# 32 instead of 24 attention score units formed ahead, in the same twelve steps

## The chip, the core and the metric

The kernel runs on one core of a Trainium2 chip. The metric is the device time of one execution in microseconds (us), as the median of several runs. The engines are TensorE (PE; its weight loads are shown apart as PEld), VectorE (DVE), ScalarE (ACT), GpSimd (POOL) and SyncE (SP, which here issues DMAs).

## What is computed

Three layers in a row, in float32: attention that keeps the 32 largest scores of each row, a mixture of eight experts whose gates are balanced by eight rounds of row and column normalisation, and a feed-forward layer with the Mish function. Cut to what matters here:

```python
# q, k, v: (2 batches, 8 heads, 576 tokens, 64)
scores = scale * np.matmul(q, k.transpose(0, 1, 3, 2))
kth = np.partition(scores, -32, axis=-1)[..., -32:-31]
scores = np.where(scores >= kth, scores, -1e9)
attn = np.exp(scores - np.max(scores, axis=-1, keepdims=True))
attn = attn / (np.sum(attn, axis=-1, keepdims=True) + 1e-09)
x = np.matmul(attn, v)             # then as 1152 tokens x 512
for e in range(8):                 # the experts, P is the balanced gate
    out += P[:, e:e + 1] * (np.maximum(x @ w1[e], 0.0) @ w2[e])
y = mish(out @ w_in) @ w_out
```

## The kernel before

The 1152 tokens are nine tiles of 128. A unit is one tile and one head (t, h), so there are 72 units, numbered 0 to 71 in order of tiles. Tiles 0 to 3 belong to the first batch, 5 to 8 to the second, tile 4 to both. A unit goes through these functions, each some steps later than the one before:

- `scores` multiplies the queries with the keys into PSUM (L227; four matmuls of 288 columns, eight for tile 4) and ScalarE copies the result to SBUF as tile `s` (L236, one copy of 576 columns), which has six buffers.
- `threshold`, two steps on, finds the 32 largest on VectorE with four MAX8 (L255) and three MATCH_REPLACE8 (L262); ScalarE takes the exponential (L273).
- `mask`, three steps on, multiplies by the mask on VectorE (L291). The first 13 units do this otherwise, with a part on GpSimd (L286, L287).
- `norm` divides by the sum: VectorE forms the reciprocal (L300, L301), ScalarE scales (L306).
- `values` turns the result on TensorE (L326, L337), ScalarE copies it (L329, L340), and TensorE multiplies with the values (L349, L356).

`attention` writes all this into a plan, a list of calls for each step; step i begins with the scores of unit i. The 24 units of `EARLY` have their scores formed ahead: all heads of tiles 2 and 3 and heads 0 to 3 of tiles 5 and 6, two in a step from step 5 to step 16, as the last calls of the step. Such a score has two PSUM banks (`mm1`, shared with the experts' first product), one for each half of 288 columns, and ScalarE copies each half (L240). The first ten units are left in SBUF tiles that are not used yet. The rest (`k >= 10`) go through an SBUF tile with two buffers, named `away`, to DRAM (L446), and are read back into an `s` tile when their turn comes (L210). `fetch`, two steps before the first unit of a half tile, loads its keys (`load_k`) and its queries (`load_q`: DMA L182, a copy to float32r on ScalarE L187, the remainder by subtraction on GpSimd L189). The query tiles `q1` and `q2` have three buffers, handed out in the order in which the loads are written.

The stages: tiles 0 and 1 alone go first. Then the experts' work on tiles 0 and 1 (c0 in the names) and tiles 2 and 3 (c1) is woven with attention on tiles 2 to 8: a generator of expert matmul groups runs, and after each group the attention generator is advanced as far as its step allows (a quarter of a step for each group). One turn ends at each `yield`; `scores` gives one where it forms scores, and none where they are there already. Last come the experts on tiles 4 to 8 (c2) and the feed-forward layer (d). An expert's piece is loaded by SP (L518, three buffers), split by ScalarE (L521) and GpSimd (L523), used by the first product (L620) and the second (L597), with hh by ScalarE (L538) and hl by VectorE (L539) between them.

TensorE's order is that of the program. The other engines' orders, SP's queue among them, are fixed when the program is built, by priorities and a planner's times. On the chip each engine works through its list in order.

Of the kernel before, what the change touches and what calls it, by code (L numbers as in the profile page):

```python
# [20 lines left out]
B, H, S, D = 2, 8, 576, 64  # L21
HG = 4
# [22 lines left out]
LAG2 = 2  # L45
AHEAD = 2
POOL_UNITS = 13
EARLY = [(t, h) for t in (2, 3) for h in range(H)] + [(t, h) for t in (5, 6) for h in range(HG)]
EARLY_FROM, EARLY_PER_STEP = 5, 2
HOLD, RATE = 8, 0.25  # L50
FILL_FROM = 11

# [21 lines left out]
def attention_moe_moe2(ctx: ExitStack, tc: tile.TileContext, qT, kT, vm, vt, wg, wst, w64, out):  # L74
# [74 lines left out]
    def load_k(b, h):  # L149


        raw = sp.tile([P, S], F32, tag="kraw", name=f"kraw_{b}_{h}", bufs=2)
        nc.sync.dma_start(raw, kT[b, h])
        k = kp.tile([P, S], F32R, tag="ks", name=f"ks_{b}_{h}")
        step, eng = (HS, nc.vector) if (b, h) == (0, 0) else (S, nc.gpsimd)
        for c in range(0, S, step):
            cols = slice(c, c + step)
            nc.scalar.activation(k[:, cols], raw[:, cols], AF.Copy)
            eng.tensor_sub(k[D:, cols], raw[D:, cols], k[D:, cols])
        ks[b, h] = k  # L160
# [32 lines left out]
    def queries(t, g):  # L193
        if (t, g) not in qset:
            qset[t, g] = load_q(t, g)
        return qset[t, g]

    def scores(t, h, store=None):

        if store is None and h % HG == 2:  # L200
            nt, ng = (t, 1) if h < HG else (t + 1, 0)
            if nt < NT and (nt, HG * ng) not in EARLY:
                with st("attn"):
# [200 lines left out]
    def attention():  # L404
        with st("attn"):
            load_k(0, 0)
            queries(0, 0)
            load_k(0, 1)
            wgraw = const.tile([P, NC, E], F32, name="wgraw")
            nc.sync.dma_start(wgraw, wg)  # L410
            nc.gpsimd.tensor_copy(wgs[:, :, :E], wgraw)
            nc.gpsimd.tensor_sub(wgs[:, :, E : 2 * E], wgraw, wgs[:, :, :E])
        units = [(t, h) for t in range(NT) for h in range(H)]
        plan = {}
        for u, (t, h) in enumerate(units):
            pooled = u < POOL_UNITS
            for order, (stage, delay) in enumerate(
                (
                    (scores, 0),
                    (partial(threshold, on_pool=pooled), AHEAD),  # L420
                    (partial(mask, on_pool=pooled), AHEAD + 1),
                    (partial(norm, on_pool=pooled), AHEAD + (2 if pooled else 1)),
                    (values, AHEAD + (3 if pooled else 2)),
                )
            ):
                plan.setdefault(u + delay, []).append((order, u, partial(stage, t, h)))
        stores = {}

        def early(t, h):

            k = EARLY.index((t, h))
            if k < 2:
                x = xfirst.tile([P, S], F32, tag=("xh1", "xl1")[k], name=f"early{k}")
            elif k < 10:
                name = ("xh2", "xl2")[(k - 2) // 4]
                if (k - 2) % 4 == 0:
                    stores[name] = xlast.tile([P, 4, S], F32, tag=name, name=f"early_{name}")
                x = stores[name][:, (k - 2) % 4, :]
            else:
                with st("attn"):  # L440
                    x = sp.tile([P, S], F32, tag="away", name=f"early{k}", bufs=2)
            yield from scores(t, h, x)
            if k >= 10:
                with st("attn"):
                    away[t, h] = dram.tile([P, S], F32, tag=f"away_{t}_{h}", name=f"away_{t}_{h}")
                    nc.sync.dma_start(away[t, h], live.pop(("s", t, h)))  # L446

        def fetch(t, h):
            with st("attn"):
                for b in range(t * P // S, (t * P + P - 1) // S + 1):  # L450
                    for i in range(h, h + HG):
                        if (b, i) not in ks:
                            load_k(b, i)
                queries(t, h // HG)
            yield from ()

        for k, (t, h) in enumerate(EARLY):
            step = EARLY_FROM + k // EARLY_PER_STEP
            plan[step].append((9, k, partial(early, t, h)))
            if h % HG == 0:  # L460
                plan[step - 2].append((8, k, partial(fetch, t, h)))
        for i in sorted(plan):
            runs = [run for _, _, run in sorted(plan[i], key=lambda x: x[:2])]
            blocks = 2 if i % 2 else 4
            for k, _ in enumerate(chain.from_iterable(run() for run in runs)):
                yield i + min(k + 1, blocks) / blocks
# [198 lines left out]


    at = attention()
    for _ in at:
        if live.get("done") == CHUNKS[0][-1]:
# [191 lines left out]
```

## Time and profile before

| | us |
|---|---|
| median of 3 runs | 1226.93 |
| lowest and highest | 1226.42, 1229.37 |
| the profiled execution | 1226.21 |
| its span, first to last instruction | 1224.4 |
| granted TensorE clock, mean share of full speed | 0.994 |

| engine | busy us | share of the span |
|---|---|---|
| TensorE (matmuls) | 1172.0 | 96% |
| weight loads | 1040.0 | 85% |
| VectorE | 858.1 | 70% |
| ScalarE | 652.7 | 53% |
| GpSimd | 540.1 | 44% |

The shares are means over stages that differ. A busy TensorE is not one at its peak, since matmuls are pipelined and their records overlap. The profile leaves out the numbers of buffers, so units are told apart by counting the instructions of a line in their order.

### The profile page before, as it was taken

What the parts mean: (1) busy time and instruction counts of PE and PEld (TensorE: products, weight loads), DVE (VectorE), ACT (ScalarE), POOL (GpSimd) and SP (SyncE); (2) the same over time, 40 slices, a digit from 0 to 9 for tenths busy, and PEclk for the clock granted to TensorE, in tenths of its full rate; (3) what the DMA queues carried; (4) which work ended last, traced back from release to release, by engine and by line L of the source; (5) the groups of instructions that cost most, each with busy time, mean ns of one, the idle gap of its engine ahead of it and who ended that gap; (6) DMA issues with size and microseconds to landing.
All of it is one profiled execution on the core that took longest, in us unless ns stands there. A gap on an engine that the chain in (4) does not pass through costs nothing.

```text
span 1224.4 us, 20740 instructions
## 1 busy us (share of the span) xinstructions
PE 1172.0 (96%) x7267; PEld 1040.0 (85%) x7267; DVE 858.1 (70%) x1857; ACT 652.7 (53%) x1289; POOL 540.1 (44%) x424
## 2 busy tenths in 40 slices
PE   2777999999999999999999999999999999999998
PEld 1556888988889898889899999999999998889997
DVE  7999999999999999713656867777666632323221
ACT  5786777877777777664223333333333333444432
POOL 7844778877777777773112112121121122221210
PEclk9899999999999999999999999999999999999999
DMA  8444555575655554665225655655444331233201
GB/s 257 125 136 148 177 173 174 171 227 179 212 165 157 163 158 155 198 220 159 69 82 186 197 190 166 213 182 188 138 139 154 118 98 62 94 95 113 77 27 43
DMA packets 105113, 183.18 MB, mean 150 GB/s; under 512 B 14128, under 2 KB 24624, under 8 KB 105008
## 3 DMA queue, kind: packets, MB, share of 16 engines
q1 hardware_dynamic: 103712, 180.68, 47.4%
q8 instruction: 57, 0.93, 0.3%
q10 hardware_dynamic: 1296, 1.18, 0.3%
q14 instruction: 48, 0.39, 0.1%
HBM read 158.55 MB, written 23.27 MB: 148 GB/s over the span
## 4 chain that ended last, share of the span: by engine, by line
PE 80%; DVE 15%; DMA 2%; ACT 1%; POOL 1%; issue 1%; SPq 0%; POOLq 0%; ACTq 0%
PE h_c2e L620 18%; PE y_c2e L597 18%; PE h_d L620 8%; PE y_d L597 8%; PE y_c0e L597 7%; PE h_c0e L620 7%; DVE top L255 6%; DVE w L262 5%; PE h_c1e L620 4%; PE y_c1e L597 4%; DVE em L291 2%; PE pv L349 2%; PE tr L326 1%; DMA kraw<-in_kT_dram 1%; PE sc L227 1%; PE pv L356 1%
## 5 line engine op out<-in xcount | busy, mean ns | idle before, releaser
L523 POOL TENSOR_TENSOR wl_c2e<-wraw_c2e,wh_c2e 128x512 fp32r<-128x512 f32 x64 | 84.0, 1312 | 344.3 <-ACT wh_c2e L521 344.3
L523 POOL TENSOR_TENSOR wl_c0e<-wraw_c0e,wh_c0e 128x512 fp32r<-128x512 f32 x128 | 171.6, 1356 | 53.7 <-ACT wh_c0e L521 50.8
L523 POOL TENSOR_TENSOR wl_c1e<-wraw_c1e,wh_c1e 128x512 fp32r<-128x512 f32 x128 | 172.7, 1373 | 51.2 <-ACT wh_c1e L521 48.2
L521 ACT ACTIVATE wh_c2e<-wraw_c2e 128x512 fp32r<-128x512 f32 x128 | 81.0, 633 | 172.9 <-PE y_c2e L597 100.6
L255 DVE MAX8 top<-w 128x8 f32<-128x576 f32 x216 | 158.2, 750 | 0.8
L620 PE MATMUL h_c2e<-xh,wh_c2e 128*128 128x320 f32 x512 | 158.2, 309 | 0.0
L620 PE MATMUL h_c2e<-xl,wh_c2e 128*128 128x320 f32 x512 | 158.0, 309 | 0.0
L620 PE MATMUL h_c2e<-xh,wl_c2e 128*128 128x320 f32 x512 | 158.0, 309 | 0.0
L539 DVE SCALAR_TENSOR_TENSOR hl_c2e<-h_c2e,hh_c2e 128x320 fp32r<-128x320 f32 x128 | 62.6, 489 | 98.1 <-ACT hh_c2e L538 97.9
L597 PE MATMUL y_c2e<-wh_c2e,hh_c2e 128*128 128x512 f32 x320 | 126.9, 397 | 0.0
L597 PE MATMUL y_c2e<-wh_c2e,hl_c2e 128*128 128x512 f32 x320 | 125.7, 393 | 0.0
L597 PE MATMUL y_c2e<-wl_c2e,hh_c2e 128*128 128x512 f32 x320 | 125.1, 391 | 0.0
L523 POOL TENSOR_TENSOR wl_d<-wraw_d,wh_d 128x512 fp32r<-128x512 f32 x32 | 41.4, 1294 | 161.0 <-ACT wh_d L521 161.0
L521 ACT ACTIVATE wh_c0e<-wraw_c0e 128x512 fp32r<-128x512 f32 x128 | 80.5, 629 | 52.6 <-PE y_c0e L597 21.0
L262 DVE MATCH_REPLACE8 w<-top,w 128x576 f32<-128x576 f32 x144 | 106.7, 743 | 0.0
L558 DVE TENSOR_TENSOR hl_d<-mg_d,hh_d 128x320 fp32r<-128x320 f32 (+1 forms) x48 | 31.6, 658 | 96.0 <-ACT hh_d L557 96.0
L620 PEld LDWEIGHTS h_c2e<-xl,wh_c2e 128*128 128x128 f32 x512 | 96.1, 188 | 2.7
L620 PEld LDWEIGHTS h_c2e<-xh,wh_c2e 128*128 128x128 f32 x512 | 96.0, 188 | 2.3
L620 PEld LDWEIGHTS h_c2e<-xh,wl_c2e 128*128 128x128 f32 x512 | 96.0, 188 | 0.0
L538 ACT ACTIVATE hh_c2e<-h_c2e 128x320 fp32r<-128x320 f32 x128 | 54.9, 429 | 76.5 <-PE h_c2e L620 75.4
L521 ACT ACTIVATE wh_c1e<-wraw_c1e 128x512 fp32r<-128x512 f32 x128 | 80.1, 628 | 28.7 <-PE y_c1e L597 12.3
L521 ACT ACTIVATE wh_d<-wraw_d 128x512 fp32r<-128x512 f32 x64 | 40.4, 632 | 95.8 <-PE y_d L597 40.9
(170 smaller groups left out, 3313.4 us busy)
## 6 DMA issues: line engine op xcount, KB each, us to landing
wraw_c0e<-in_wst_dram SPq DMA_DIRECT2D x128, 256.0 KB, 3.0
wraw_c1e<-in_wst_dram SPq DMA_DIRECT2D x128, 256.0 KB, 3.0
wraw_c2e<-in_wst_dram SPq DMA_DIRECT2D x128, 256.0 KB, 3.0
cx<-in_w_dram SPq DMA_DIRECT2D x32, 512.0 KB, 4.0
wraw_d<-w SPq DMA_DIRECT2D x64, 256.0 KB, 2.6
yd<-ysp SPq DMA_DIRECT2D x32, 256.0 KB, 3.6
yb<-yd SPq DMA_DIRECT2D x32, 256.0 KB, 3.2
w<-cc SPq DMA_DIRECT2D x32, 256.0 KB, 3.4
```

Of the source, the lines that this page charges most:

```text
L227: nc.tensor.matmul(halves[half], q[:, h % HG, :], ks[b, h][:, half * HS : (half + 1) * HS], start=(i == 0), stop=(i == len(terms) - 1),)
L255: top8 = nc.vector.max(g, src)
L262: nc.vector.match_replace(w, g, src, NEG)
L291: nc.vector.scalar_tensor_tensor(em, s, kth, e, op0=ALU.is_ge, op1=ALU.mult, accum_out=sm)
L349: nc.tensor.matmul(pv[i * D : (i + 1) * D, pair, c0:c1], vmain[b, pair][:, i, c, :], live["at", i][:, c, c0:c1], start=(c == 0), stop=False,)
L521: nc.scalar.activation(hi, raw, AF.Copy)
L523: eng.tensor_sub(lo, raw, hi)
L538: nc.scalar.activation(h, ps, AF.Relu)
L539: live["hl"] = nc.vector.scalar_tensor_tensor(l, ps, 0.0, h, op0=ALU.max, op1=ALU.subtract)
L558: nc.vector.tensor_sub(l, g, h)
L597: nc.tensor.matmul(y, h[:, j * P : (j + 1) * P], w, start=(f == 0 and k == 0), stop=(f == nf - 1 and k == 2),)
L620: nc.tensor.matmul(ps, w[:, c * P : (c + 1) * P], x[:, c, c0 : c0 + m], start=(k == 0), stop=(k == 3 * NC - 1),)
```

## The change

Heads 0 to 3 of tiles 7 and 8 join the list, which makes 32 units. They are spread over the same twelve steps, 5 to 16, by 3, 3, 2 in turns instead of two in each. The new ones have `k >= 24`, so they go to DRAM as units 10 to 23 do. The keys that they need are those of tiles 5 and 6; two more query loads come to the first stage, and are no longer made later. The steps of the older units shift: `fetch` for tile 5 is called in step 9 instead of 11, for tile 6 in step 10 instead of 13, and for tiles 7 and 8 in steps 12 and 13.

```diff
-EARLY = [(t, h) for t in (2, 3) for h in range(H)] + [(t, h) for t in (5, 6) for h in range(HG)]
-EARLY_FROM, EARLY_PER_STEP = 5, 2
+EARLY = [(t, h) for t in (2, 3) for h in range(H)] + [(t, h) for t in (5, 6, 7, 8) for h in range(HG)]
+EARLY_FROM, EARLY_STEPS = 5, 12
@@ attention
         for k, (t, h) in enumerate(EARLY):
-            step = EARLY_FROM + k // EARLY_PER_STEP
+            step = EARLY_FROM + k * EARLY_STEPS // len(EARLY)
             plan[step].append((9, k, partial(early, t, h)))
             if h % HG == 0:
                 plan[step - 2].append((8, k, partial(fetch, t, h)))
```

## Rows read from the trace of the kernel before

**Rows 1.** The page: span, then busy tenths in 40 equal slices.

```profile
span 1224.4 us, 20740 instructions
...
PE   2777999999999999999999999999999999999998
...
DVE  7999999999999999713656867777666632323221
```

**Rows 2.** Stretches: us; busy PE, PEld, DVE, ACT, POOL (instructions); clock; DMA.

```profile
33.00:57.00 24.00, 16.82 (x85) 13.46 (x86) 23.77 (x59) 17.86 (x40) 22.51 (x17) 0.80 0.52 150
...
57.00:100.00 43.00, 31.21 (x216) 25.05 (x215) 43.00 (x113) 37.66 (x91) 18.18 (x16) 0.95 0.43 142
...
380.00:500.00 120.00, 119.05 (x863) 106.26 (x862) 119.06 (x282) 89.67 (x178) 90.92 (x67) 1.00 0.53 161
```

**Rows 3.** TensorE's waits, 120 us to the end: total us, times, longest; first and last.

```profile
PE tr L337 <- ACT at L329: 0.8, 1, 0.8
...
PE h_c1e L620 <- DVE hl_c1e L539: 0.2, 1, 0.2
```

**Rows 4.** Lines L306 and L326: duration ns min/median/max, first and last start.

```profile
L306 ACT ACTIVATE em<-em,r x72: 758/768/819, 29.8 to 511.9; 128x576 f32<-128x576 f32 x72
...
L326 PE MATMUL tr<-ident,em x288: 270/272/476, 30.6 to 522.6; 128*128 128x128 f32 x144
```

**Rows 5.** Timeline: start us, us, engine, line, operation; units 39 and 55.

```profile
288.39 0.77 ACT L306 ACTIVATE em<-em,r 128x576 f32<-128x576 f32 x1
...
289.70 0.66 PE L326 MATMUL tr<-ident,em 128*128 128x128 f32 x4 [0.24 <-ACT at L329]
...
394.18 0.76 ACT L306 ACTIVATE em<-em,r 128x576 f32<-128x576 f32 x1
...
410.48 0.60 PE L326 MATMUL tr<-ident,em 128*128 128x128 f32 x4
```

**Rows 6.** The chain that ended last, 490 to 500 us: start us, us, what.

```profile
493.22 0.54 PE sc L227 x4
...
496.97 0.53 PE sc L227 x4
```

**Rows 7.** The page's DMA issues: count, KB each, median us to landing.

```profile
s<-away SPq DMA_DIRECT2D x14, 288.0 KB, 4.1
```

**Rows 8.** ScalarE's groups, 57 to 100 us: count | busy us, mean ns | idle before.

```profile
L240 ACT ACTIVATE early<-sc 128x288 f32<-128x288 f32 x28 | 10.6, 417 | 1.1 <-ACT early L240 0.7 <-PE sc L227 0.3
...
L187 ACT ACTIVATE q<-qraw 128x512 fp32r<-128x512 f32 x7 | 4.4, 625 | 0.0
```

**Rows 9.** TensorE's longest wait, 57 to 100 us: total us, times, longest.

```profile
PE sc L227 <- ACT early L240: 8.7, 9, 2.2
```

**Rows 10.** Timeline: copies of two early units of one step.

```profile
81.05 0.72 ACT L240 ACTIVATE early<-sc 128x288 f32<-128x288 f32 x2
...
83.07 0.69 ACT L240 ACTIVATE early<-sc 128x288 f32<-128x288 f32 x2
```

**Rows 11.** Timeline: a query load's two halves.

```profile
68.96 0.62 ACT L187 ACTIVATE q<-qraw 128x512 fp32r<-128x512 f32 x1
...
69.72 2.74 POOL L189 TENSOR_TENSOR q<-qraw,q 128x512 fp32r<-128x512 f32 x2 [3.57 <-ACT q L187]
```

**Rows 12.** Timeline: the end of the first stage.

```profile
90.59 0.65 ACT L236 ACTIVATE s<-sc 128x576 f32<-128x576 f32 x1
...
91.82 0.75 DVE L255 MAX8 top<-s 128x8 f32<-128x576 f32 x1
...
97.79 0.84 PE L227 MATMUL sc<-ks,q 128*128 128x288 f32 x4 [0.86 <-ACT early L240]
...
100.90 1.58 PE L349 MATMUL pv<-at,vm 128*64 128x128 f32 x16 [0.84 <-ACT at L329]
...
104.74 0.66 PE L326 MATMUL tr<-ident,em 128*128 128x128 f32 x4 [1.41 <-ACT em L306]
...
107.40 0.36 PE L620 MATMUL h_c0e<-xh,wh_c0e 128*128 128x256 f32 x1
```

## The prediction

> **What bounds the kernel now.** I read the page first, then the stretches, then who waited for whom on TensorE, then the chain. The slices [rows 1] show two regimes. Up to slice 4 (about 107 us) VectorE is full and TensorE is not; from then to the end TensorE is full, and VectorE beside it as far as slice 16 (about 500 us). The stretches say it in numbers [rows 2]: from 57 to 100 us VectorE is busy 43.00 of 43, ScalarE 37.66, TensorE 31.21; from 380 to 500 us TensorE has 119.05 of 120 and VectorE 119.06. Two engines at 99% do not tell which sets the pace, so I looked at waits: from 120 us to the end TensorE has five kinds of wait, from 0.8 us down to 0.2, together 2.6 us [rows 3]. It has also a reserve against VectorE. The last of the 72 normalisations (L306) begins at 511.9 and lasts 0.77; the last of the four transposes that need it (L326) starts at 522.6 [rows 4]. VectorE's and ScalarE's result is there some 9.5 us early. For tile 6's last head (unit 55, counted in order) it is 410.48 less 394.94, 15.5 us [rows 5]. So after 107 us TensorE sets the time, with VectorE 10 to 15 us ahead; before it VectorE does, with ScalarE close behind.
>
> **What leaves the long stretch.** The eight units are heads 0 to 3 of tiles 7 and 8. Each is four matmuls of 288 columns. On the chain a unit takes 0.54 and 0.53 us from its first matmul to the next work [rows 6] (their "busy" adds up to more, since pipelined matmuls overlap). 8 x 0.535 = 4.3 us come off TensorE between about 390 and 470 us. Eight copies to SBUF and two query loads leave ScalarE and GpSimd there too, for which TensorE did not wait; I count them at nothing. If VectorE were not ahead, none of the 4.3 would come through: the reserve of 9.5 to 15.5 us is the cover. What is late next is VectorE.
>
> **What comes back there.** Eight reads of 288 KB on SP's queue replace the copies. A read waits for a free one of six `s` buffers, and behind it in SP's queue stand the weight loads. The fourteen such reads of before are of the same kind, land in a median 4.1 us [rows 7], and left no wait on TensorE for weights [rows 3]. Bounds: a gain is excluded, since nothing waited for the copies; a weight load held up by one read is 4 us late at most, with three buffers ahead of it. I take nothing, by the fourteen.
>
> **What the moved scores call forth.** A score that returns at once yields no turn to the weaving of attention into the experts, so the transposes of odd units come earlier by about a step; and four stored units arrive together, so VectorE interleaves more units and the older ones end later. Before shows this at heads 4 to 7 of tile 4, while the four stored units of tile 5 were due: the normalisation of unit 39 begins at 288.39, its transposes at 289.70 [rows 5], a reserve of 0.5 us where unit 55 has 15.5. So such a group takes some 15 us of reserve for a moment, and the units ahead of tiles 7 and 8 have about that. Bounds: 0, to 4.3 us of waits (the whole gain); I take 0.3, since the wait at unit 39 was 0.24 [rows 5], and since a TensorE that arrives later (next part) gives reserve back.
>
> **What enters the first stage.** Steps 5 to 16 take 3, 3, 2 units by turns instead of 2: up to step 8 that is 11 instead of 8, from step 9 on 21 instead of 16. ScalarE pays most: a unit is two copies of 0.417 us, 0.83, and the two query loads (now here) 0.625 each [rows 8]. From 33 to 57 us three units add 2.5 us to 17.86 of 24 [rows 2]: covered. From 57 to 100 us five units and two query copies add 4.15 + 1.25 = 5.4 us to 37.66 of 43: 43.06, no idle time left. GpSimd gets two subtractions of 1.3 us and has room (18.18 of 43). SP gets eight more writes, each of which waits in its queue for two copies.
>
> Does the end of the stage move? TensorE works in order, and its early scores have two PSUM banks for two halves: the second unit of a step waits for the copies of the first. From 57 to 100 us it waited 8.7 us for these copies alone [rows 9], so here it walks at ScalarE's pace. Lower bound: the 5.4 us fill the 5.3 idle us, shift 0. Middle: ScalarE keeps the share it reached, 37.66 / 43 = 0.876, and 5.4 / 0.876 = 6.2 us are added. Upper bound: each of five third units costs TensorE a whole round trip, as from the copies at 81.05 to those at 83.07 [rows 10], 2.0 us, so 10; and a query buffer adds to it. There are three; the loads' order becomes (5,0) before (1,1), so (5,0) gets the buffer that head 3 of tile 1 still reads in step 11, and is itself wanted in step 11. The trace shows what refilling costs: the copy begins at 68.96, GpSimd's part at 69.72 and it is 1.3 us long [rows 11]; some 2 us, with one unit's transposes (0.5) to cover them, so 1.5. Lag at most 11.5.
>
> The tail takes some of it back. Between the last early score (97.79) and the experts' first matmul (107.40) TensorE waits 0.84 + 1.41 = 2.2 us for the last units [rows 12]; a late TensorE finds them done. Shift = 6.2 - 2.2 = 4.0 us; from both sides 0 to 9.3. I take the middle, for the stretch reached no more than 0.876 while TensorE stood waiting for it. VectorE should lose less: it takes a unit 0.6 us after its score is copied (90.59 + 0.65, then 91.82), but that unit is transposed only at 104.74 [rows 12], 13 us later for some 6 us of work (43 us make about 7.5 units), so older work lies beside it.
>
> **The sum.** Profiled execution 1226.21 (span 1224.4 and 1.8 around it): -4.3 + 4.0 + 0.3 = 0.0, so 1226.2. The median of the runs shown is 0.7 above the profiled one: 1226.9, in round numbers 1227.
>
> Here a rule speaks against the change. The Trainium skill (Perfetto Trace Analysis, Identifying the Most-Contended Engine) takes occupancy as a fair measure of how close VectorE is to its limit, and not for TensorE's matmuls. By it VectorE's 119.06 of 120 would make it the engine to relieve from 380 to 500 us, and taking scores off TensorE there would give nothing. The reserve of 9.5 to 15.5 us speaks against it, as far as 4.3 us go.
>
> **The rivals.** *Faster:* the copies fit in ScalarE's idle time and the shift is 0: 1226.9 - 4.3 = 1222.6. For it: 5.3 us idle against 5.4. Against: engines in order that wait for each other seldom fill every gap. 0.18.
>
> *Slower, first stage:* round trips and the query buffer set TensorE's lag, 11.5 us, shift 9.3. It decides once the lag passes the 2.2 us of tail and the 4.3 us of gain, 6.5 us. Time 1226.9 - 4.3 + 9.3 = 1231.9. For it: the waits for copies [rows 9]. Against: ScalarE's backlog shrinks when TensorE is slower. 0.20.
>
> *VectorE is the pace from 380 to 500 us:* waits before the transposes take the 4.3 back, and the first stage's 4.0 stay: 1226.9 + 4.0 = 1230.9. For it: unit 39. Against: no wait over 0.8 us now. 0.09.
>
> That the change does not do what it says: the units can only be moved, but a read that lands late would make VectorE wait where ScalarE's copy came in time; this is inside the third rival's price.
>
> **How the numbers follow.** Forecast 1227 (0.53), faster 0.18, the two slower ones 0.29. The measurement tells about 0.3%, 3.7 us, so "same" is 1223.2 to 1230.6; the faster case lies just below it, the slower ones just above. Range 1222 to 1233, a microsecond beyond the outer cases.
>
> **What would show it.** Right: L236 falls from 48 copies to 40 and L240 rises from 48 to 64; the experts' first matmul starts near 111 us instead of 107.4; ScalarE is above 90% from 57 us to the last early copy; from there to the end TensorE's way is some 4 us shorter, with waits near 3 us. Wrong towards faster: first matmul at 107 to 108. Wrong towards slower: past 114 us, with longer waits for early copies or query loads; or waits of several us before L326 near 400 and 465 us. The forecast fails altogether if the engines' static order, which is planned anew for the whole program, comes out different elsewhere.

## The result and the profile after

The changed kernel takes 1236.28 us (median of 6 runs, 1232.91 to 1237.51); the kernel before, run beside it, 1227.73 (6 runs, 1226.42 to 1229.37). The ratio is 1.0070, 95% interval 1.0057 to 1.0083: slower by 8.6 us. I had forecast 1227 with a range of 1222 to 1233, so the time lies outside it, on the slower side. The profiled execution of the changed kernel is the fastest of its six, 1232.91 (span 1231.1); the trace shows 6.7 us of the 8.6.

The page of the changed kernel, as in [rows 1], with TensorE's granted clock below:

```profile
span 1231.1 us, 20808 instructions
...
PE   3777999999999999999999999999999999999998
...
DVE  7999999899999999823656777777666632323221
PEclk9888999999999999999999999999999999999999
```

The stretches of [rows 2] again: us; busy PE, PEld, DVE, ACT, POOL (instructions); granted clock; DMA share; GB/s.

```profile
33.00:57.00 24.00, 18.50 (x94) 13.98 (x92) 23.58 (x60) 19.65 (x45) 23.22 (x18) 0.86 0.52 146
57.00:100.00 43.00, 30.96 (x175) 24.60 (x174) 40.98 (x99) 34.85 (x82) 16.98 (x14) 0.84 0.40 136
380.00:500.00 120.00, 119.10 (x874) 105.97 (x873) 119.41 (x291) 89.36 (x175) 93.79 (x69) 1.00 0.61 192
```

From 57 to 100 us more work was planned, and less gets done: TensorE runs 175 matmuls where it ran 216, VectorE 99 instructions for 113, ScalarE 82 for 91. ScalarE's busy time falls from 37.66 to 34.85 of 43 us. The stage did not fill up; it became slower.

The end of the first stage on TensorE, against [rows 12] (timeline: start us, us, engine, line, operation, what it waited for):

```profile
104.23 0.53 PE L227 MATMUL sc<-ks,q 128*128 128x288 f32 x2 [2.03 <-ACT early L240]
105.05 2.29 PE L227 MATMUL sc<-ks,q 128*128 128x288 f32 x6 [0.29 <-ACT early L240]
...
112.45 0.83 PE L227 MATMUL sc<-ks,q 128*128 128x288 f32 x4 [0.35 <-ACT early L240]
113.12 1.04 PE L326 MATMUL tr<-ident,em 128*128 128x128 f32 x8
...
115.21 1.58 PE L349 MATMUL pv<-at,vm 128*64 128x128 f32 x16 [0.94 <-ACT at L329]
...
120.14 0.37 PE L620 MATMUL h_c0e<-xh,wh_c0e 128*128 128x256 f32 x1
```

The same stretch on ScalarE: unit 15's score is copied, and later an early copy waits for a store:

```profile
101.82 0.65 ACT L236 ACTIVATE s<-sc 128x576 f32<-128x576 f32 x1
...
110.56 0.71 ACT L240 ACTIVATE early<-sc 128x288 f32<-128x288 f32 x2 [1.56 <-DMA away<-early]
```

And on VectorE, unit 15's first maximum:

```profile
102.51 0.76 DVE L255 MAX8 top<-s 128x8 f32<-128x576 f32 x1
```

The experts' first matmul starts at 120.14 in place of 107.40, 12.7 us late. Unit 15's score is copied at 101.82 in place of 90.59, and VectorE takes it at once. From the experts' first matmul to the end of the span the way is 1231.1 - 120.1 = 1111.0 us; before it was 1224.4 - 107.4 = 1117.0. So the trace reads: +12.7 in the first stage, -6.0 behind it.

Behind it, TensorE's waits from 120 us to the end, as in [rows 3]:

```profile
PE tr L326 <- ACT at L329: 1.6, 4, 0.9
PE h_c0e L620 <- DVE hl_c0e L539: 1.1, 1, 1.1
PE cs L493 <- DVE gate L489: 0.2, 1, 0.2
```

L306 and L326, with the columns of [rows 4]:

```profile
L306 ACT ACTIVATE em<-em,r x72: 756/769/808, 28.2 to 518.1; 128x576 f32<-128x576 f32 x72
...
L326 PE MATMUL tr<-ident,em x288: 270/272/474, 29.0 to 528.8; 128*128 128x128 f32 x144
```

The timeline at unit 55, as in [rows 5]:

```profile
414.12 0.76 ACT L306 ACTIVATE em<-em,r 128x576 f32<-128x576 f32 x1
...
415.43 0.66 PE L326 MATMUL tr<-ident,em 128*128 128x128 f32 x4 [0.90 <-ACT at L329]
```

And the reads among the DMA issues, as in [rows 7]:

```profile
s<-away SPq DMA_DIRECT2D x22, 288.0 KB, 4.1
```

The waits sum to 2.9 us against 2.6. Unit 55, now followed by four stored units, has its reserve cut to 415.43 - 414.88 = 0.55 us, and what TensorE then waits for, 0.90 us, is ScalarE's copy of transposes (L329). The last unit's reserve is as before. The 22 reads land in the same median 4.1 us as the 14 did.

### The profile page after: what moved, and what is told of

It is laid out like the page before. It is cut to its first block, busy times and chain, and to the rows that moved or that the text cites. A ratio compares the mean times of both kernels' runs of the same rounds, so it can differ in the third digit from the quotient of the medians.

```text
span 1231.1 us, 20808 instructions
## 1 busy us (share of the span) xinstructions
PE 1180.0 (96%) x7267; PEld 1045.0 (85%) x7267; DVE 858.9 (70%) x1857; ACT 656.7 (53%) x1298; POOL 545.3 (44%) x425
## 4 chain that ended last, share of the span: by engine, by line
PE 89%; DVE 3%; ACT 3%; DMA 3%; POOL 1%; issue 1%; SPq 0%; ACTq 0%; POOLq 0%
PE h_c2e L620 18%; PE y_c2e L597 18%; PE h_d L620 8%; PE y_d L597 8%; PE h_c0e L620 7%; PE y_c0e L597 7%; PE h_c1e L620 7%; PE y_c1e L597 7%; PE pv L349 3%; PE tr L326 2%; PE sc L227 2%; DMA kraw<-in_kT_dram 1%; DVE top L255 1%; PE pv L356 1%; DVE w L262 1%
## 5 line engine op out<-in xcount | busy, mean ns | idle before, releaser
L523 POOL TENSOR_TENSOR wl_c0e<-wraw_c0e,wh_c0e 128x512 fp32r<-128x512 f32 x128 | 174.3, 1373 | 48.3 <-ACT wh_c0e L521 41.7
L620 PE MATMUL h_c2e<-xh,wh_c2e 128*128 128x320 f32 x512 | 158.3, 309 | 0.0
L620 PE MATMUL h_c2e<-xl,wh_c2e 128*128 128x320 f32 x512 | 157.9, 308 | 0.0
L620 PE MATMUL h_c2e<-xh,wl_c2e 128*128 128x320 f32 x512 | 157.8, 308 | 0.0
L620 PEld LDWEIGHTS h_c2e<-xh,wh_c2e 128*128 128x128 f32 x512 | 96.0, 188 | 2.5
L620 PEld LDWEIGHTS h_c2e<-xl,wh_c2e 128*128 128x128 f32 x512 | 96.0, 188 | 2.3
L227 PE MATMUL sc<-ks,q 128*128 128x288 f32 x320 | 69.3, 350 | 29.6 <-ACT early L240 12.1
L620 PEld LDWEIGHTS h_c2e<-xh,wl_c2e 128*128 128x128 f32 x512 | 96.0, 188 | 0.0
```

The costliest lines, as they stand in the source:

```text
L227: nc.tensor.matmul(halves[half], q[:, h % HG, :], ks[b, h][:, half * HS : (half + 1) * HS], start=(i == 0), stop=(i == len(terms) - 1),)
L523: eng.tensor_sub(lo, raw, hi)
L620: nc.tensor.matmul(ps, w[:, c * P : (c + 1) * P], x[:, c, c0 : c0 + m], start=(k == 0), stop=(k == 3 * NC - 1),)
```

## The experiments

Unless another base is named, an edit is made to the changed kernel. A "third unit" is the third early unit of a step that has three; there are eight. "First matmul" is the experts' first matmul (L620) in the run's profiled execution.

**Gain and price apart.** First the eight units' forming is left out of the kernel before.

```
+SKIPPED = [(t, h) for t in (7, 8) for h in range(HG)]
...
+        at_ = (t - 2, h) if (t, h) in SKIPPED else (t, h)
+        if at_ in away:
...
+                nc.sync.dma_start(s, away[at_])
```

> The kernel before, without forming the scores of heads 0 to 3 of tiles 7 and 8 at all: the stored scores of tiles 5 and 6 are read a second time in their place, so these eight units work on other scores. The first stage is that of before. If TensorE is the pace from 380 to 500 us: 4.3 us under before, 1223.4. If VectorE is: no change, 1227.7. With waits before the transposes near 400 and 465 us: between, 1224 to 1227.

1223.33 us, ratio 0.9972 [0.9961, 0.9983]: -3.4 us. First matmul 108.9, from there to the end 1111.5. The gain is there, though VectorE is as busy as before (119.54 of 120 us from 380 to 500 us). Then the price without the gain:

```
...
-        if (t, h) in away:
+        if (t, h) in away and t < 7:
```

(with the queries of tiles 7 and 8 loaded a second time)

> The changed kernel, but the eight new units, formed ahead and stored, are formed again in their place (with their query loads), and the stored ones are never read. Pays the whole price in the first stage and gains nothing after it: if gain and price simply add, 4.3 us over the changed kernel, 1240.6; the experts' first matmul near 120 us as in the changed kernel. If the late start hides something later, less.

1237.88, ratio 1.0089 [1.0069, 1.0109]: +10.9 us; first matmul 121.4. Gain and price add up to 7.5 of the measured 8.6 us, which the intervals allow.

**Is it the number of units, or their density?** Only 24 units, as before, but in nine steps:

```
+EARLY = [(t, h) for t in (2, 3) for h in range(H)] + [(t, h) for t in (5, 6) for h in range(HG)]
+EARLY_FROM, EARLY_STEPS = 5, 9
```

> The 24 units of before at the density of the changed kernel: 3, 3, 2 in turns over nine steps instead of two in each of twelve. If the number of units in a step is what hurts (round trips through two PSUM banks), TensorE falls behind in these nine steps by some 5 us and has three empty steps to catch up: first expert matmul 108 to 110 us, time 1228 to 1230. If the total amount of work hurts, as before: 1227.7. If a query buffer wanted in the step that frees it hurts, it is here too (tile 5 in step 11): up to 2 us.

1233.87, ratio 1.0058 [1.0039, 1.0077]: +7.1 us with not one matmul or copy more than the kernel before. First matmul 115.9. From 57 to 100 us (columns as above):

```profile
57.00:100.00 43.00, 32.49 (x171) 26.27 (x171) 39.69 (x97) 32.74 (x79) 18.08 (x16) 0.74 0.42 141
```

ScalarE is busy 32.74 of 43 us, and TensorE needs 32.49 us for 171 matmuls where before it needed 31.21 for 216. So more work is not needed for the cost; three to a step suffice, and they cost more than the 1228 to 1230 us that I had named. One thing comes with them in this run as in the change: `fetch` is called for tile 5 in step 9 and for tile 6 in step 10, in place of 11 and 13. No run has three to a step without these sooner loads.

Next all 32, two to a step, over sixteen steps (`EARLY_STEPS` 16):

> The 32 units, but two to a step over sixteen steps, so that no step has a third. Where a step with two early units takes what it took before, the first stage ends its two tiles as before (first matmul of the experts near 107 us in place of 120.1), and the last eight units stand in the steps behind it, beside the experts, where they cost TensorE about what they save later: 1224 to 1229 us. Were the price one of the number of early units, wherever they stand (stores, reads, ScalarE's copies): 1233 us or more. By the theory of the third unit (24 units in 9 steps have 6 thirds and cost 7.1 us, the 8 units with no gain have 8 thirds and cost 10.9 us: 1.2 to 1.4 us for each) the price is zero.

1235.22, ratio 1.0061 [1.0045, 1.0077]. ScalarE's timeline where unit 15's score is copied:

```profile
90.24 0.65 ACT L236 ACTIVATE s<-sc 128x576 f32<-128x576 f32 x1
```

TensorE's timeline at the first matmul:

```profile
112.60 0.37 PE L620 MATMUL h_c0e<-xh,wh_c0e 128*128 128x256 f32 x1
```

And TensorE's wait for early copies from 105 to 180 us (total us, times, longest):

```profile
PE sc L227 <- ACT early L240: 4.8, 4, 2.1
```

With two to a step unit 15 is copied at 90.24 us, as in the kernel before (90.59), and its normalisation is on time as well (103.92 before). The transposes that need it are not (104.74 before):

```profile
103.86 0.78 ACT L306 ACTIVATE em<-em,r 128x576 f32<-128x576 f32 x1
...
108.89 1.05 PE L326 MATMUL tr<-ident,em 128*128 128x128 f32 x4
```

So half of my theory held, up to unit 15's score. Behind it the early units that are left stand ahead of the last transposes in TensorE's order, with 2.1 of the 4.8 us of waits, and the first matmul is 5.2 us late. The last of them stand beside the experts, where I had expected them to cost no more than they save; the way from the first matmul to the end is 1120.4 us, longer than the kernel before's 1117.0. The time is in the range of the rival that I had named, a price of each early unit wherever it stands. Beginning two steps sooner instead (`EARLY_FROM, EARLY_STEPS = 3, 14`):

> The 32 units over fourteen steps, beginning two steps sooner: four steps of a third unit in place of eight. Theory of the third unit: 4 x 1.2 to 1.4 us of price less the gain of 3.4 us: 1228 to 1230 us, with the first matmul of the experts near 112 to 114 us. Rival, that the amount of work in the first stage sets its length: as the change, 1235 to 1238 us. A second rival: the sooner start takes keys and ScalarE from the first units, which at 22 to 37 us wait for their keys, and costs more there: over 1238 us.

1236.28, ratio 1.0068; first matmul 122.2. The time lies in the range of the first rival. The trace shows what the second one named: TensorE's waits from 20 to 60 us are now for keys (1.9 us in the changed kernel). So this run cannot tell what four third units in place of eight are worth.

```profile
PE sc L227 <- POOL ks L159: 16.7, 2, 11.7
```

**One resource at a time.** Each of the next takes away one thing on which TensorE or ScalarE was seen to wait. Four tiles instead of two for the stores:

```
+                    x = sp.tile([P, S], F32, tag="kraw" if k >= 16 and k % 2 else "away", name=f"early{k}", bufs=2)
```

> The changed kernel with four SBUF tiles instead of two for the units on their way to DRAM (from unit 16 of the list on, every second one uses the two tiles through which keys come in). ScalarE's waits for a store to land (2.8 us in the changed kernel) go. If they set the lag: 5 us or more come back, 1231 or less. If not: 1234 to 1237.

1236.19, ratio 1.0069. ScalarE's waits from 33 to 115 us; first the one for stores in the changed kernel:

```profile
ACT early L240 <- DMA away<-early: 2.8, 3, 1.6
```

The same view of this run:

```profile
ACT em L306 <- DVE r L301: 3.8, 3, 1.6
...
ACT early L240 <- DMA away<-early: 0.9, 1, 0.9
```

The wait for stores goes from 2.8 to 0.9 us, a wait for VectorE of 3.8 us that the changed kernel does not have there takes its place, and the first matmul is at 120.1 as before. Query buffers of their own (the queries of tiles 5 and 8 in `yp` tiles):

> The changed kernel, but the queries of tiles 5 and 8 go to two tiles that are free in the first stage, so no query load waits for a buffer that is read in the step that needs it. If the two late query loads (copies at 74.8 and 101.3 us in the changed kernel) set the lag: 3 to 5 us come back, 1231 to 1233. If not: 1235 to 1237.

1237.47, ratio 1.0072; first matmul 120.1. Every other early unit through the PSUM banks `sc` of the ordinary scores, with one copy in place of two:

> The changed kernel, but every second early unit is formed in the two banks of the main scores and leaves PSUM in one copy of 576 columns instead of two of 288. If the round trip through the two banks sets TensorE's lag, most of the 13 us of the first stage go, first expert matmul at 108 to 112 us, time 1224 to 1229. If it is the landing of the stores, the query buffers or the clock, the first matmul stays past 116 us and the time above 1232.

1237.18, ratio 1.0080; first matmul 122.5. The same in the kernel before, as a control:

> The kernel before (24 units, two in each step) with every second early unit in the banks of the main scores and one copy for it. In before VectorE sets the end of the first stage, so faster early scores should bring 0 to 1 us: 1226.7 to 1227.7. If the round trips cost time there too, TensorE's lag of 4 to 7 us in the middle of the stage goes and up to 2 us come back.

1227.88, ratio 1.0001. Every other early unit in the two banks that hold the odd transposes (`tag=("mm1", "mm2")[store_k % 2]`):

> The change, with every other early unit's scores formed in the two PSUM banks that hold the odd transposes, so that TensorE can run two units ahead of ScalarE's copies in place of one. If the two banks are what ties TensorE to the copies: TensorE's waits for early copies between 57 and 115 us (14, 11.2 us) fall to under 4 us and the time to 1226 to 1231 us. If it is ScalarE's order (the copies stand behind exponentials and norms that wait for VectorE), waits move from copies to copies and the time stays at 1235 to 1238 us.

1240.27, ratio 1.0104, worse. The waits of scores for early copies fall from 10.8 us in the changed kernel (13 times in this window; the 11.2 named above belong to a longer one) to 7.2, and the transposes wait for the same copies instead (57 to 115 us):

```profile
PE tr L326 <- ACT early L240: 8.8, 3, 4.5
PE sc L227 <- ACT early L240: 7.2, 10, 1.5
```

The first of the three placed right behind the step's own scores (order 0.5 in place of 9):

> The change, with the first of the three units of a step placed right behind the step's own scores, ahead of its transposes and products, instead of all three last. If the lag comes from three hand-offs of TensorE and ScalarE in a row at the end of a step, it falls: 1227 to 1233 us, the score of unit 15 written before 99 us in place of 102.5. If it is the number of early units in a step, wherever in it they stand: 1235 to 1239 us.

1237.78, ratio 1.0084; first matmul 125.6. Another place within the step brings nothing back.

**The clock.** TensorE's granted clock from 57 to 100 us fell from 0.95 to 0.84. Unread matmuls in the gaps ahead of each further early unit of a step raise it:

```
+            if k and step_of(k) == step_of(k - 1):
...
+                idle = ps_m.tile([P, 512], F32, tag="mm2", name=f"idle{k}", bufs=2)
+                for _ in range(4):
+                    nc.tensor.matmul(idle, ks[0, 0][:, :P], ks[0, 0][:, :512], start=True, stop=True)
```

> The changed kernel with four extra matmuls of 512 columns, whose result nobody reads, before each early unit that is not the first of its step (20 times, 0.9 us each at full clock). If the lowered clock (0.82 granted from 57 to 113 us) is a cause of its own, the granted clock rises to 0.95 or more there and the time falls by 2 to 5 us although TensorE has 18 us more work in the stage. If it only follows from the waits, the time is the same or higher.

The stretch from 57 to 100 us:

```profile
57.00:100.00 43.00, 34.92 (x217) 28.93 (x217) 41.24 (x102) 34.36 (x81) 17.84 (x15) 0.94 0.40 135
```

The clock is 0.94 there, near the 0.95 of before the change; the time 1237.43, ratio 1.0070, is that of the change, and the first matmul comes at 122.6. With half the filler:

> The change with two unread 128x512 matmuls (in place of four) in the gap ahead of each further early unit of a step. With four the granted clock was 0.91 to 0.99, TensorE had 18 us more work, and the time was that of the change. If the low clock carries a large part of the lag, half of the filler keeps most of the clock and frees some 9 us of TensorE: first matmul of the experts near 113 to 117 us, 1229 to 1233 us. If the clock is a companion of the lag and not its cause: 1234 to 1238 us with the first matmul at 119 us or later.

1240.37, ratio 1.0112; clock 0.86 in that stretch, first matmul 122.5. Half of the filler hardly raised the clock, so this run says nothing about it. In the full one the clock came back and the time did not; but its unread matmuls are work for TensorE too, some 18 us by the estimate above, and what the clock gave and what they took cannot be told apart. Two runs from above help, the one with four store tiles and the one with query buffers of its own, in this order:

```profile
57.00:100.00 43.00, 30.02 (x174) 24.14 (x174) 40.99 (x102) 34.41 (x81) 17.88 (x15) 0.87 0.38 127
57.00:100.00 43.00, 31.44 (x175) 25.20 (x175) 40.99 (x99) 34.73 (x82) 18.73 (x16) 0.80 0.41 142
```

The clock is 0.87 in one and 0.80 in the other, and in both the first matmul is at 120.1. So the lag does not follow the clock from run to run; a share of its own is not excluded. The Trainium skill (TensorE: Matmul & The Clock Gate, HAM oscillation — how this bites in real kernels) advises restructuring a matmul loop that waits for DMA so that TensorE keeps its full clock; here TensorE waited for another engine, and a clock kept up by unread matmuls won nothing.

**Whose part is it?** Now the third units in pieces. Only their copies (of a stored tile, in place of the scores):

```
+            if third:
...
+                for half in range(2):
+                    nc.scalar.activation(x[:, half * HS : (half + 1) * HS], stores["first"][:, half * HS : (half + 1) * HS], AF.Copy)
...
+            else:
+                yield from scores(t, h, x)
```

> The change, but the third unit of each step that has three is not formed: ScalarE copies a stored tile of the same size twice by halves in its place, and stores and reads stay (the output is of other scores there). TensorE's part and the hand-off are gone, ScalarE's part and the transfers stay. If ScalarE's time (8 units of two copies) or the transfers make the lag, it stays: first matmul of the experts at 116 us or later, 1233 to 1238 us. If it is TensorE's time or the hand-offs between the two: at 112 us or sooner, 1223 to 1229 us.

1237.68, ratio 1.0094 [1.0074, 1.0114]: +10.8 us, no less than the change, without one of their matmuls. The stretch from 57 to 100 us:

```profile
57.00:100.00 43.00, 30.41 (x168) 24.82 (x167) 41.52 (x107) 36.00 (x83) 18.15 (x15) 0.75 0.41 140
```

The first matmul on TensorE's timeline:

```profile
119.28 0.37 PE L630 MATMUL h_c0e<-xh,wh_c0e 128*128 128x256 f32 x1
```

Only their matmuls (`if not third:` ahead of the copies):

> The change, but the third unit of each step that has three is formed and never copied or stored; its place later is taken by the unit ahead of it (the output is of other scores there). TensorE's part stays, ScalarE's part, the hand-off and six stores are gone. If TensorE's time in the first stage, low clock or not, makes the lag: first matmul of the experts at 116 us or later, 1233 to 1238 us. If it is ScalarE's time or the hand-offs: at 112 us or sooner, 1223 to 1229 us. With both this and the copies alone near 1225 us only the hand-offs are left.

1229.91, ratio 1.0026 [1.0015, 1.0037]: +3.0 us, where the change has +8.6. The gain of 3.4 us is in both, so the price is 6.4 against 12.0, about half. The stretch again:

```profile
57.00:100.00 43.00, 31.15 (x195) 24.87 (x193) 41.57 (x102) 35.05 (x81) 19.41 (x18) 0.92 0.41 133
```

The first matmul:

```profile
114.73 0.36 PE L628 MATMUL h_c0e<-xh,wh_c0e 128*128 128x256 f32 x1
```

Without five of the stores:

> The change, with the stores of five of the eight third units left out (the unit stored ahead of them is read in their place, so the output is of other scores there); forming and copying stay. If the stores (copies that wait for a tile's landing, transfers beside the reads) make the lag: first matmul of the experts at 114 us or sooner, 1228 to 1231 us. If not: 1234 to 1238 us.

1237.73, ratio 1.0089; first matmul 122.5: these stores are not it. I expected one piece to carry the lag and the other to be free of it, or both to be free. Neither came: of the change's 12.7 us at the first matmul the copies alone keep 11.9 (119.3 less 107.4) and the matmuls alone 7.3, so the two overlap, and ScalarE's copies are the larger. Both runs keep the two added query loads and the sooner `fetch`; what they have in common may lie there.

**Is it ScalarE's load, then?** Other work of more than the same size is taken off ScalarE: early query roundings and seven normalisations go to GpSimd.

```
+                if (t, HG * g) in EARLY and t >= 3:
+                    nc.gpsimd.tensor_copy(q1[:, i : i + step, :], raw[:, i : i + step, :])
+                else:
+                    nc.scalar.activation(q1[:, i : i + step, :], raw[:, i : i + step, :], AF.Copy)
...
+            if 9 <= t * H + h <= 15:
+                nc.gpsimd.tensor_scalar(em, em, r, None, op0=ALU.mult)
+            else:
+                nc.scalar.activation(em, em, AF.Copy, scale=r)
```

> The change, with other work taken off ScalarE between 50 and 112 us and given to GpSimd, which is idle for half of that stretch: the rounded copies of six early query loads (6 x 0.63 us) and the normalisations of units 9 to 15 (7 x 0.77 us), together 9.2 us, against 8 x 2 x 0.41 = 6.6 us that the third units' copies add. If ScalarE's queue is what makes the lag (copies alone kept it, matmuls alone kept little of the time): first matmul of the experts at 108 to 113 us in place of 120.1, 1224 to 1230 us. If the lag is from TensorE's part or from the order of the hand-offs: 117 us or later, 1233 to 1238 us. GpSimd takes a normalisation about twice as long; if that latency decides, it is slower than the change, over 1238 us.

1232.49, ratio 1.0051 [1.0038, 1.0065]: +6.3 us, where the change has +8.6. The two intervals overlap, so the 2.3 us between them are not shown. The stretch from 57 to 100 us:

```profile
57.00:100.00 43.00, 30.77 (x179) 24.84 (x180) 38.37 (x96) 30.65 (x75) 26.84 (x23) 0.80 0.42 142
```

The first matmul:

```profile
119.19 0.36 PE L626 MATMUL h_c0e<-xh,wh_c0e 128*128 128x256 f32 x1
```

ScalarE's waits from 33 to 112 us:

```profile
ACT em L312 <- DVE r L304: 6.8, 4, 2.3
ACT early L243 <- DMA away<-early: 4.2, 5, 1.0
```

ScalarE is busy 30.65 of 43 us, far less than in the kernel before (37.66), and the first matmul is still at 119.19. The time given to ScalarE went into its waits: it stands ahead of a normalisation until VectorE's factor is there (6.8 us; 2.6 before the change, and no such wait in the changed kernel from 33 to 115 us). The relief has a price too: a normalisation takes 1.73 us on GpSimd in place of 0.77. The control, the same relief in the kernel before:

> The same relief of ScalarE in the kernel before (24 units). VectorE is full there from 57 to 100 us and sets the pace, so ScalarE's relief gives little: 1224 to 1228 us, first matmul at 105 to 108 us. If ScalarE holds the kernel before back too, as TensorE's 8.7 us of waits for early copies could mean: under 1224 us. If GpSimd's longer normalisations decide: over 1228 us.

1228.32, ratio 1.0010 [1.0002, 1.0019]; first matmul 109.4. There the relief gives nothing, with VectorE full (43.00 of 43 us); it costs 1.3 us, a little past the range that I had named for it, on the side of GpSimd's longer normalisations.

**What the runs settle, and what not.** The price lies in the first stage, 10.9 us when it is alone. It comes without added work where the early units stand three to a step (+7.1 us with 24 units); two to a step put the lag off behind unit 15's score and do not spare it. Of the third units, ScalarE's copies alone keep nearly all of the lag and the matmuls alone over half. Five of the stores, the query buffers, the pair of PSUM banks and ScalarE's load were each taken away or eased, and the lag stayed; in three of these runs another wait stood in the place of the one removed.

Which engine is late can be read unit by unit. Unit 12's normalisation on ScalarE and its first transposes on TensorE, in the kernel before:

```profile
96.52 0.76 ACT L306 ACTIVATE em<-em,r 128x576 f32<-128x576 f32 x1
...
98.46 0.60 PE L326 MATMUL tr<-ident,em 128*128 128x128 f32 x4
```

Its normalisation in the changed kernel:

```profile
94.50 0.78 ACT L306 ACTIVATE em<-em,r 128x576 f32<-128x576 f32 x1
```

The transposes of unit 12 start there at 113.12 (shown above). The normalised unit is ready 2.0 us sooner than before and is taken 14.7 us later. Unit 8, counted in the same way, is normalised 4.7 us sooner and transposed 9.6 us later. So up to unit 14 it is not VectorE that is late (its reciprocals, by 0.9 us at most). TensorE comes late by its own list, by 1.2 us at unit 4's transposes and by 14.7 at unit 12's. Unit 15 alone, whose score was late, has its reciprocal 5.8 us late (109.38 for 103.63), and its normalised result too waits for TensorE, from 111.9 to 117.5 us.

What is left is TensorE's list of small steps, each early score behind ScalarE's copies of the one ahead, and these in ScalarE's queue among its other work. This is argued from the trace and by exclusion: no run removes the hand-offs alone. Open are the share of the clock, the share of the sooner loads, and that of the order. The order on each engine is planned anew for each program, and it did change: counted in the trace, unit 15's first maximum is VectorE's 201st instruction before the change and its 218th after, while the unit's last (the reciprocal) is the 234th and 232nd. VectorE was given more old work ahead of the new unit. Whether that order follows from the late scores or helps to make them late was not tried, since the edits move both. No kernel that does the whole computation came out faster than the one before.

## Why the prediction was wrong

*What bounds the kernel:* right. The gain of 3.4 us without the price shows that TensorE sets the time behind the first stage, with VectorE at 119 of 120 us beside it. The rival "VectorE is the pace" falls. The Trainium skill (Perfetto Trace Analysis, Identifying the Most-Contended Engine) would have the engine with the highest occupancy relieved first, here VectorE; for this stretch the run does not agree, since work taken off TensorE gave 3.4 us.

*The gain, 4.3 us:* right within what can be told. 3.4 us in the run that has it alone, between 2.1 and 4.8 by its interval. The 6.0 us in the trace of the change are not gain alone: in the runs with the price alone and with 24 units in nine steps, which save nothing there, the way behind the first matmul is 1114.2 and 1114.7 us, so a late start by itself shortens it by 2.8 and 2.3. Of this 1.1 are waits at the start of the experts (h_c0e for hl and xl, 2.2 us before, 1.1 after).

*The reads at nothing, the waits at 0.3:* right. 4.1 us to land, as before; waits from 120 us on 2.9 against 2.6. The reserve at unit 55 was cut from 15.5 to 0.55 us as foreseen.

*The first stage, 4.0 us:* this is the step that failed, in the term "ScalarE keeps the share it reached, 0.876". The shift measured 12.7 us in the trace. I had treated the added copies as work that is poured in at a fixed rate. In the run ScalarE's share fell to 34.85 / 43 = 0.81, and in the relief run, with 9.2 us of other work off ScalarE and a share of 0.71, the first matmul was only 1.0 us sooner: the share was a result and not a limit. What set the end was TensorE, which came to units that lay ready (unit 12: 2.0 us sooner ready, 14.7 us later taken). The last early copy ends at 114.7 us against 100.4, a lag of 14.3, where I had 6.2 for the middle and 11.5 for the upper bound. The upper bound was closer, and of the kind that the runs point to (a round trip for each third unit), but it counted only five third units, since the three up to step 8 were called covered: eight at 2.0 us make 16. Its 1.5 us for a query buffer did not show: with buffers of their own for tiles 5 and 8 the first matmul stayed at 120.1.

*The tail, 2.2 us back:* right in kind: of the two waits at the end (0.84 and 1.41) the second is gone, and 14.3 - 12.7 = 1.6 us came back.

*"VectorE should lose less":* right in kind. Its reciprocal for unit 14 is 0.9 us late (102.42 for 101.53), that for unit 15 5.8, where the first matmul is 12.7 late.

*The marks I named:* L236 fell from 48 copies to 40 and L240 rose from 48 to 64. "Past 114 us" was the mark for slower, and it came. Its other half, "longer waits for early copies", is there only faintly: from 33 us to the first matmul these waits sum to 15.4 us for 13.8, and the longest is 2.6 for 2.2; the lag stands in the trace as busy time (last section). "ScalarE above 90% from 57 us to the last early copy" was the mark for right, and it was 44.75 of 57.7 us, 78%. The last sentence, on the order planned anew, named what the runs could not take apart.

*The rival:* "slower, first stage" had the place of the price and the round trips, with 1231.9 us and a chance of 0.20, and was still 4.4 us short. It was the better forecast on what the trace showed: TensorE's waits for early copies [rows 9] already stood there as the longest ones, so TensorE's list, and not ScalarE's share, was the thing to price.

## What to carry to other kernels

An engine that is busy 88% of a stage need not have room for another 12%: here three engines hand work round in order, and when 5.4 us of copies and query loads were to join ScalarE's 37.66 of 43, its share went down. Where the trace shows one engine waiting for another's small steps, price an added unit by a whole round trip for every place where it is added, and keep the share of busy time as the lower bound. In this case the round trips are an upper bound: 8 x 2.0 = 16 us against a lag of 12.7 at the first matmul, and 6 x 2.0 = 12 against 8.5 for 24 units in nine steps. And test a price apart from its gain: 3.4 us of gain and 10.9 us of price were each plain once they ran alone.

## What the runs showed of the hardware

TensorE's granted clock fell behind a wait for a hand-off. In the changed kernel from 60 to 68 us the stretches read (columns as above):

```profile
60.00:64.00 4.00, 1.39 (x12) 1.16 (x10) 3.39 (x10) 3.92 (x9) 1.72 (x2) 0.96 0.19 74
64.00:68.00 4.00, 3.80 (x13) 3.12 (x14) 3.93 (x11) 3.15 (x9) 1.27 (x1) 0.50 0.40 129
```

TensorE's timeline in them and just behind:

```profile
63.93 1.67 PE L227 MATMUL sc<-ks,q 128*128 128x288 f32 x4 [2.61 <-ACT early L240]
65.80 2.29 PE L227 MATMUL sc<-ks,q 128*128 128x288 f32 x8 [0.20 <-ACT early L240]
...
72.36 1.37 PE L227 MATMUL sc<-ks,q 128*128 128x288 f32 x8 [0.29 <-ACT early L240]
```

After a stretch with TensorE busy 1.39 of 4 us, ended by a wait of 2.61 us for an early copy, the clock is 0.50, the level of 1.2 GHz, and eight score matmuls take 2.29 us in place of 1.37. So a wait can look like work afterwards. The stretches from 33 us to the experts' first matmul, before the change and after:

```profile
33.00:107.40 74.40, 52.86 (x344) 42.04 (x345) 74.10 (x190) 60.26 (x140) 41.97 (x34) 0.91 0.47 146
33.00:120.14 87.14, 65.39 (x375) 51.23 (x373) 83.51 (x203) 68.37 (x158) 45.10 (x36) 0.84 0.50 158
```

TensorE is idle 21.5 us before the change and 21.7 after, and 12.5 of the 12.7 us stand as busy time, where the eight units alone are some 4.3. Read so, the clock looks like the cause. Against it stand the two runs with 0.87 and 0.80 and the same first matmul, and the filled run with 0.94 and the same time, in which the unread matmuls hide what the clock gave. The runs leave open how much of the lag the clock carries.
